# Moving the loads of V and of the weights from SyncE with casts on compute engines to casting DMAs issued by GpSimd

## The chip, the cores and the metric

One core of one Trainium2 chip. The metric is the device time of one execution in microseconds (us), the median over the executions of a run. Traces are of one profiled execution each. Seven of the fourteen traces (e3b, e4, e5, e6, e8, e9, e10) lack the records of 40 to 43 of the 1152 dense matmuls. Where a sum over all matmuls is quoted, it is of traces that have all 1152. Medians in the text are over all runs of a kernel; e2, e3 and e5 have one slow run of four, and for them the median of the fast three is given too.

## The reference

```python
q_d, k_d, v_d = (t.reshape(B, H, S // 4, 4, D).mean(axis=3) for t in (q, k, v))
out_up    = np.repeat(softmax_attention(q_d, k_d, v_d), 4, axis=2)     # pooled attention
mask      = np.abs(pos[:, None] - pos[None, :]) < 4
out_local = softmax(where(mask, scale * q @ k.T, -1e9)) @ v            # banded attention
x = (out_up + out_local).transpose(0, 2, 1, 3).reshape(B * S, H * D)   # 4608 x 512
h = x @ w_in                                                           # 512 x 2048
return (h - tanh(h)) @ w_out                                           # 2048 x 512
```

B = 8, H = 8, S = 576, D = 64. Inputs and output are float32; the kernel computes its matmuls in bf16. Heads are handled in pairs, 4 pairs to a batch, so 32 pairs: pairs 0 to 3 are batch 0, pairs 4 to 7 batch 1.

## The kernel before

The kernel records every piece of work as an operation (engine, estimated time, reads, writes, priority) and then lets its own scheduler place all of them, before the chip sees anything. So each engine's instruction order is fixed when the kernel is built. An operation with the keys it reads or writes is ordered after the ones that wrote them. `op("POOL", ...)` is GpSimd, `op("SP", ...)` is SyncE's queue, `op("DMA", ...)` stands for a transfer.

```python
def load(ns, fn, keys, cost, pri):
    op("SP", ns, fn, writes=list(keys) + ["queue", ("q", keys[0])], pri=pri)
    op("DMA", cost, None, reads=[("q", keys[0])], writes=keys, pri=pri)

def load_v(p):                     # V of a pair: two heads, 128 x 5 rows of 64 floats each
    ...
    for i in range(2):
        def issue(...):
            nc.sync.dma_start(out=t[:, i], in_=win(-4, 128, 5))       # t: fp32 staging tile
        load(1000, issue, [("vst", s, i)], T_V, -30)                  # a key for each head

def load_w(src, dst, name, f, stage, keys):                           # a 1 MB piece of weights
    ...                                                               # fp32 into borrowed space,
    load(600, issue, keys, T_W, -30)                                  # then four casts
    for c in range(4):
        P.choice([... for eng, ns, fn in CAST], reads=keys, writes=[(name, f, c)], ...)

def prep_v(p):                                                        # the cast of V
    P.choice([... tensor_copy(out=vw[w][:, 2 * jj:2 * jj + 2, :, 0:64], in_=vst[s]) ...],
             reads=[("vst", s, 0), ("vst", s, 1)], writes=[("vw", w, jj)], pri=10 * p - 12)

load_qk(0)
for p in range(NP):                # NP = 4 pairs of batch 0
    if p + 1 < NP:
        load_qk(p + 1)
    load_v(p)
...                                # then w_in; w_out between the loads of pairs 4 to 7
```

While PE (TensorE) would be idle before its first dense matmul, the emitter fills in matmuls on a constant tile ("filler"); these compute nothing.

The softmax here doesn't subtract the row's maximum and nothing guards it: scores larger than these inputs give would overflow.

## Time and profile before

| | before |
|---|---|
| median, 2 runs | 346.85 us (346.81 to 346.89) |
| profiled span (a further run, 345.75 us) | 343.9 us |
| first out-matmuls of pairs 0 / 2 | 17.55 / 24.61 us |
| first dense matmul | 30.45 us |
| first out-matmuls of pairs 4 to 7 | 46.8, 54.0, 61.4, 68.1 us |
| PE time without useful matmuls, to 50 us / to the end | 21.4 / 38.1 us |

"Out-matmuls" are those of attention probabilities with V (`ps_ox<-vw,E`); "dense" are the 1152 matmuls of 128x512 of the two weight layers. The last row is worked out from the trace: each matmul that isn't filler is counted at the time that its columns take (512 columns: 0.216 us, from runs of eight dense matmuls that take 1.73 us), and what is missing from the clock time is unused. Short matmuls take longer than their columns (the 320 out-matmuls take 63 ns each, 65 columns are 27 ns), so the absolute figures are too large.

From the page of the kernel before (busy us and share; busy tenths of 40 slices; the queue; instruction groups; an issue):

```profile
PE 322.8 (94%) x2502; PEld 162.9 (47%) x2502; DVE 225.0 (65%) x370; ACT 227.0 (66%) x368; POOL 155.1 (45%) x200
PE   4777999989999999989999799999999999999995
POOL 5644555646689625668976686783000000000000
q1 hardware_dynamic: 99278, 60.30, 68.0%
L351 POOL CAST vw<-vst 128x640 bf16<-128x640 f32 x32 | 26.2, 818 | 7.0 <-DMA vst<-in_v_dram 5.6
vst<-in_v_dram SPq DMA_DIRECT2D x62, 160.0 KB, 5.1
```

PE is nearly full from the fifth slice (34 us) to the end, so the time is PE's work plus what the first slices lose. V is cast 32 times on GpSimd for 0.82 us each; all data comes on one queue.

The timeline of PE before (start, length, what, and in brackets the idle time before it and what ended it):

```profile
17.55 0.33 PE L536 MATMUL ps_ox<-vw,E 128*128 128x65 bf16 x5
...
24.61 0.32 PE L536 MATMUL ps_ox<-vw,E 128*128 128x65 bf16 x5 [0.25 <-ACT vd L396]
...
30.45 2.75 PE L617 MATMUL ps_hy<-xT,w_in_sb 128*128 128x512 bf16 x12 [1.20 <-DVE xT L597]
```

V is there when PE wants it: none of these waits on it. Busy time by stretch in the crowded middle of the kernel (us PE, PEld, DVE, ACT, POOL, then granted clock, DMA share, GB/s):

```profile
100.00:220.00 120.00, 114.52 (x978) 57.92 (x977) 98.52 (x152) 98.35 (x150) 85.63 (x97) 1.00 1.01 223
```

GpSimd is busy 85.6 of 120 us, 71%.

### The profile page before, as it was taken

The numbers are of one execution on the slowest core, as the hardware profiler recorded it, in microseconds if no ns is written. First come the engines' busy times: TensorE is split into PE (matmuls) and PEld (weight loads), VectorE is DVE, ScalarE is ACT, GpSimd is POOL, SyncE is SP. The second block draws the span as 40 slices with busy tenths as digits, with TensorE's granted clock in tenths as the row PEclk, the third lists the DMA queues.
The fourth block names the chain that finished last, engine by engine and source line by source line (L and its number), as shares of the span: only waits on it lengthen the run. The fifth ranks groups of instructions, "written<-read, shape, count | busy, mean of one in ns | idle before, by whom it ended". The sixth has DMA issues, their size and how long they took to land.

```text
span 343.9 us, 6722 instructions
## 1 busy us (share of the span) xinstructions
PE 322.8 (94%) x2502; PEld 162.9 (47%) x2502; DVE 225.0 (65%) x370; ACT 227.0 (66%) x368; POOL 155.1 (45%) x200
## 2 busy tenths in 40 slices
PE   4777999989999999989999799999999999999995
PEld 2453555545565554434454344545444444444442
DVE  3787784579989878888887868876533433344300
ACT  2885996578878949878888687985443444344411
POOL 5644555646689625668976686783000000000000
PEclk9899999999999999999999999999999999999999
DMA  7999999985779884999999999834201000100021
GB/s 210 273 393 349 328 355 306 294 266 152 176 196 234 199 215 95 216 256 200 253 232 268 237 255 215 192 78 66 57 30 63 30 30 32 61 30 33 30 90 64
DMA packets 99310, 60.72 MB, mean 177 GB/s; under 512 B 77774, under 2 KB 82382, under 8 KB 99278
## 3 DMA queue, kind: packets, MB, share of 16 engines
q1 hardware_dynamic: 99278, 60.30, 68.0%
q8 instruction: 19, 0.31, 0.4%
q14 instruction: 13, 0.11, 0.1%
HBM read 42.46 MB, written 9.44 MB: 151 GB/s over the span
## 4 chain that ended last, share of the span: by engine, by line
PE 69%; DVE 8%; DMA 8%; issue 5%; POOL 4%; ACT 3%; SPq 2%; POOLq 0%; ACTq 0%; DVEq 0%
PE ps_hy L617 29%; PE ps_hy L644 29%; DMA qT<-qr 4%; PE ps_ts L476 2%; DVE ln L554 2%; PE ps_ox L536 2%; DMA vst<-in_v_dram 2%; DVE E L512 2%; PE ps_ts L441 2%; DMA qkn<-in_k_dram 2%; PE ps_ox L543 1%; SPq L291 1%; POOL half L457 1%; DMA lT<-ln 1%; PE ps_ox L389 1%
## 5 line engine op out<-in xcount | busy, mean ns | idle before, releaser
L617 PE MATMUL ps_hy<-xT,w_in_sb 128*128 128x512 bf16 x576 | 145.1, 379 | 1.2 <-DVE xT L597 1.2
L644 PE MATMUL ps_hy<-w_out_sb,gT 128*128 128x512 bf16 x576 | 142.6, 379 | 0.0
L628 DVE TENSOR_TENSOR gT<-ps_hy,u 128x512 bf16<-128x512 f32 x144 | 96.5, 686 | 65.8 <-ACT u L625 64.0
L625 ACT ACTIVATE u<-ps_hy 128x512 f32<-128x512 f32 x144 | 84.1, 601 | 67.8 <-PE ps_hy L617 67.3
L644 PEld LDWEIGHTS <-gT 128*128 128x128 bf16 x576 | 54.4, 98 | 63.3
L617 PEld LDWEIGHTS <-w_in_sb 128*128 128x128 bf16 x576 | 52.8, 98 | 59.8 <-issue 1.3
L457 POOL TENSOR_TENSOR half<-qk 128x576 f32<-128x576 bf16 x28 | 32.5, 1160 | 19.4 <-ACT qk L445 10.9
L432 ACT COPY qk<-qT 128x576 bf16<-128x576 bf16 x32 | 38.0, 1216 | 0.0
L509 ACT ACTIVATE E<-ps_ts 128x960 bf16<-128x960 f32 x32 | 30.9, 972 | 9.4 <-PE ps_ts L476 9.1
L554 DVE TENSOR_TENSOR ln<-ps_ox,r 128x896 bf16<-128x896 f32 x32 | 34.9, 1090 | 1.0
L416 POOL CAST qr<-qkn 128x576 bf16<-128x576 f32 x31 | 22.8, 735 | 24.7 <-PE ps_ts L441 11.1
L512 DVE TENSOR_TENSOR E<-E,mask 128x960 bf16<-128x960 bf16 x32 | 28.0, 879 | 8.2 <-ACT E L509 8.1
L655 ACT COPY y<-ps_hy 128x512 f32<-128x512 f32 x36 | 21.2, 589 | 17.9 <-PE ps_hy L644 17.6
L351 POOL CAST vw<-vst 128x640 bf16<-128x640 f32 x32 | 26.2, 818 | 7.0 <-DMA vst<-in_v_dram 5.6
L416 DVE CAST qr<-qkn 128x576 bf16<-128x576 f32 x32 | 23.7, 744 | 6.4 <-DMA qkn<-in_k_dram 3.9
L536 PE MATMUL ps_ox<-vw,E 128*128 128x65 bf16 x320 | 20.1, 194 | 3.3 <-DVE E L525 1.8
L462 POOL TENSOR_TENSOR qkd<-half 128x288 bf16<-128x288 f32 x30 | 21.4, 714 | 2.9 <-DVE r L552 1.7
L372 POOL TENSOR_TENSOR v<-v 72x512 f32<-72x512 f32 x16 | 20.9, 1309 | 1.2 <-DMA v<-in_v_dram 0.2
L536 PEld LDWEIGHTS <-E 128*128 128x128 bf16 x320 | 16.3, 98 | 10.8 <-DVE E L512 2.7
L445 ACT COPY qk<-ps_ts 128x1152 bf16<-128x1152 bf16 x16 | 18.0, 1126 | 3.9 <-PE ps_ts L441 3.9
L376 POOL TENSOR_TENSOR vp<-v 72x256 bf16<-72x256 f32 x16 | 11.7, 732 | 17.5 <-PE ps_ox L543 16.6
L476 PEld LDWEIGHTS <-qk 64*128 64x128 bf16 x320 | 10.2, 95 | 18.5 <-issue 16.9
(74 smaller groups left out, 260.2 us busy)
## 6 DMA issues: line engine op xcount, KB each, us to landing
vst<-in_v_dram SPq DMA_DIRECT2D x62, 160.0 KB, 5.1
qkn<-in_q_dram SPq DMA_DIRECT2D x32, 288.0 KB, 3.6
qkn<-in_k_dram SPq DMA_DIRECT2D x32, 288.0 KB, 4.5
out_dram<-y SPq DMA_DIRECT2D x36, 256.0 KB, 3.0
v<-in_v_dram SPq DMA_DIRECT2D x16, 288.0 KB
gT<-in_moe_w_in_dram SPq DMA_DIRECT2D x4, 1024.0 KB, 6.2
xT<-in_moe_w_out_dram SPq DMA_DIRECT2D x8, 256.0 KB, 6.4
gT<-in_moe_w_out_dram SPq DMA_DIRECT2D x2, 1024.0 KB, 8.1
```

The source lines that it names most:

```text
L351: P.choice([(eng, ns, lambda fn=fn: fn(out=vw[w][:, 2 * jj:2 * jj + 2, :, 0:64], in_=vst[s])) for eng, ns, fn in CAST_V[p >= NEARLY]], rea ...
L416: P.choice([(eng, ns, lambda dst=dst, srt=srt, fn=fn: fn(out=dst, in_=srt)) for eng, ns, fn in REORDER[p >= NEARLY][h]], reads=[("qkn", sn ...
L432: op("ACT", 600, lambda i=i: A.copy(out=full[:, i].rearrange("p (g a) -> p g a", a=A9), in_=qT[s].rearrange("p a (g i) -> p i g a", i=2)[: ...
L457: eng.tensor_tensor(out=half, in0=four[:, :, :, 0:2], in1=four[:, :, :, 2:4], op=ALU.add)
L509: op("ACT", 870, lambda: A.activation(out=e1, in_=ps[:, :, 0:480], func=AF.Exp, scale=SCALE), reads=ts, writes=[("E", s, 0)], pri=pri)
L512: op("DVE", 700, lambda: V.tensor_tensor(out=e1, in0=e1, in1=mask[:, 0:480].unsqueeze(1).to_broadcast([128, 2, 480]), op=ALU.mult), reads= ...
L536: T.matmul(po[:, hh, 65 * t:65 * t + 65], E[s][:, c:c + 128], vw[w][:, 2 * jj + hh, t, :], start=True, stop=True)
L554: op("DVE", 1010, lambda: V.tensor_tensor(out=ln[s].rearrange("p n (h d) -> p h n d", d=D), in0=blocks[:, :, :, 0:64], in1=r[s].unsqueeze( ...
L617: T.matmul(ps_hy[slot], w_in_sb[:, dc, fc * 128:(fc + 1) * 128], xT[dc][:, kb * 512:kb * 512 + 512], start=(dc == 0), stop=(dc == N_DC - 1))
L625: op("ACT", 490, lambda: A.activation(out=u[us], in_=ps_hy[slot], func=AF.Tanh), reads=[("hy", slot)], writes=[("u", us)], pri=-1)
L628: op("DVE", 620, lambda: V.tensor_tensor(out=gT[g][:, fc, :], in0=ps_hy[slot], in1=u[us], op=ALU.subtract), reads=[("hy", slot), ("u", us) ...
L644: T.matmul(ps_hy[slot], gT[g][:, fc, ts * 128:ts * 128 + 128], w_out_sb[:, fc, :], start=(fc == 0), stop=(fc == N_FF - 1))
```

## The change

The intent is to spare the casts of V and weights (26 us of GpSimd for V), the staging tiles, and half of the bytes that V and weights write, and to leave SyncE to q, k, transposes and stores. The Trainium skill (DMA: Bandwidth & Descriptors, SWDGE vs HWDGE vs iDMA) has a cast during a DMA as a feature of GpSimd-issued DMAs alone, so they all move to GpSimd's instruction order.

```diff
-    NQKN, NVST, NVW = 4, 5, 3
+    NQKN, NVW = 4, 4
-    vst = fixed("vst", [128, 2, NT, 64], FP32, NVST)
 ... load_v:
-                    nc.sync.dma_start(out=t[:, i], in_=win(-4, 128, 5))
+                    GP.dma_start(out=t, in_=win(-4, 128, 5))          # t: slice of bf16 vw
-            load(1000, issue, [("vst", s, i)], T_V, -30)
+            op("POOL", 1000, issue, writes=[("vw", w, jj), ("vq", p, i)], pri=10 * p - 40)
+            op("DMA", T_V, None, reads=[("vq", p, i)], writes=[("vw", w, jj)], pri=-30)
 ... load_w (w_out alike; the casts go):
+                GP.dma_start(out=dst[:, :, 512 * f:512 * f + 512],
+                             in_=src[:, 512 * f:512 * f + 512].rearrange(
+                                 "(c p) f -> p c f", p=128))
+        op("POOL", 1000, issue, reads=[("q", after)], writes=keys + [("wq", name, f)],
+           pri=W_PRI)
+        op("DMA", T_W, None, reads=[("wq", name, f)], writes=keys, pri=-30)
-    def prep_v(p): ...
 ... order of the loads:
+        load_w(moe_w_in, w_in_sb, "w_in", f, ("qkn", 3, 1))
 ...
+        if 0 <= nl[0] - NP - 1 < 4:
+            load_w(moe_w_out, w_out_sb, "w_out", nl[0] - NP - 1,
+                   ("qkn", (nl[0] - 1) % NQKN, 1))
```

Both heads of a pair now write the *same* key `("vw", w, jj)`, so to the scheduler the second head's load follows the landing of the first. And a weight may be issued as soon as a load of q and k has been *issued* (`("q", after)`).

More of the change, by code (lines that the diff above doesn't have):

```diff
@@ L296, in load_v @@
     def load_v(p):
-        b, j, s = p // NP, p % NP, p % NVST
-        t = vst[s]
+        b, j, w, jj = p // NP, p % NP, (p // 2) % NVW, p % 2
         for i in range(2):
@@ L302, in load_v @@
             base = v[b, h]
+            t = vw[w][:, 2 * jj + i, :, 0:64]
             def win(tok, n, nt, base=base):
@@ L306, in win, with issue @@
                                ap=[[D, n], [QW * D, nt], [1, D]])
-            def issue(h=h, i=i, win=win):
+            def issue(h=h, win=win, t=t):
                 if b == 0 and h == 0:
-                    nc.sync.dma_start(out=t[4:128, i, 0, :], in_=v[b, h, 0:124, :])
-                    nc.sync.dma_start(out=t[:, i, 1:5, :], in_=win(QW - 4, 128, 4))
+                    GP.dma_start(out=t[4:128, 0, :], in_=v[b, h, 0:124, :])
+                    GP.dma_start(out=t[:, 1:5, :], in_=win(QW - 4, 128, 4))
@@ L312, in issue @@
                 elif b == B - 1 and h == H - 1:
-                    nc.sync.dma_start(out=t[0:100, i, 4, :], in_=v[b, h, 476:576, :])
-                    nc.sync.dma_start(out=t[:, i, 0:4, :], in_=win(-4, 128, 4))
+                    GP.dma_start(out=t[0:100, 4, :], in_=v[b, h, 476:576, :])
+                    GP.dma_start(out=t[:, 0:4, :], in_=win(-4, 128, 4))
                 else:
-                    nc.sync.dma_start(out=t[:, i], in_=win(-4, 128, 5))
+                    GP.dma_start(out=t, in_=win(-4, 128, 5))
@@ L317, in load_v, with clear @@
             if (b, h) in ((0, 0), (B - 1, H - 1)):
-                def clear(h=h, i=i):
-                    part = t[0:32, i, 0, :] if h == 0 else t[96:128, i, 4, :]
+                def clear(h=h, t=t):
+                    part = t[0:32, 0, :] if h == 0 else t[96:128, 4, :]
                     V.memset(part, 0.0)
-                op("DVE", 100, clear, writes=[("vst", s, i)], pri=-99)
-            load(1000, issue, [("vst", s, i)], T_V, -30)
-    def load_w(src, dst, name, f, stage, keys):
+                op("DVE", 100, clear, writes=[("vw", w, jj)], pri=-99)
@@ L326, in issue, with load_w @@
+            op("POOL", 1000, issue, writes=[("vw", w, jj), ("vq", p, i)], pri=10 * p - 40)
+            op("DMA", T_V, None, reads=[("vq", p, i)], writes=[("vw", w, jj)], pri=-30)
+    def load_w(src, dst, name, f, after):
         def issue():
             if src is moe_w_in:
-                nc.sync.dma_start(out=stage.rearrange("p (c f) -> p c f", c=4),
-                                  in_=src[:, 512 * f:512 * f + 512].rearrange(
-                                      "(c p) f -> p c f", p=128))
-            else:
-                rows = src.rearrange("(f p) n -> p f n", p=128)
-                if isinstance(stage, list):
-                    for c in range(4):
-                        nc.sync.dma_start(out=stage[c], in_=rows[:, 4 * f + c, :])
-                else:
-                    nc.sync.dma_start(
-                        out=stage.rearrange("p (c f) -> p c f", c=4),
-                        in_=rows[:, 4 * f:4 * f + 4, :])
@@ L340, in load_w @@
-        load(600, issue, keys, T_W, -30)
-        for c in range(4):
-            part = stage[c] if isinstance(stage, list) else stage[:, 512 * c:512 * c + 512]
-            to = dst[:, c, 512 * f:512 * f + 512] if src is moe_w_in else dst[:, 4 * f + c, :]
-            P.choice([(eng, ns, lambda part=part, to=to, fn=fn: fn(out=to, in_=part))
-                      for eng, ns, fn in CAST], reads=keys, writes=[(name, f, c)],
-                     pri=W_PRI + f)
-    def prep_v(p):
-        s, w, jj = p % NVST, (p // 2) % NVW, p % 2
-        P.choice([(eng, ns, lambda fn=fn: fn(
-            out=vw[w][:, 2 * jj:2 * jj + 2, :, 0:64], in_=vst[s]))
-                  for eng, ns, fn in CAST_V[p >= NEARLY]],
-                 reads=[("vst", s, 0), ("vst", s, 1)],
-                 writes=[("vw", w, jj)], pri=10 * p - 12)
+                GP.dma_start(out=dst[:, :, 512 * f:512 * f + 512],
+                             in_=src[:, 512 * f:512 * f + 512].rearrange(
+                                 "(c p) f -> p c f", p=128))
+            else:
+                GP.dma_start(out=dst[:, 4 * f:4 * f + 4, :],
+                             in_=src.rearrange("(f p) n -> p f n", p=128)
+                             [:, 4 * f:4 * f + 4, :])
@@ L357, in load_v4 @@
+        keys = [(name, f, c) for c in range(4)]
+        op("POOL", 1000, issue, reads=[("q", after)], writes=keys + [("wq", name, f)],
+           pri=W_PRI)
+        op("DMA", T_W, None, reads=[("wq", name, f)], writes=keys, pri=-30)
     def load_v4(p):
@@ L683 @@
     M2_FIRST, T_DMA, X_DMA, NEW = 16, 16, 16, 16
-    ORDER = "p0p1p2p3"
     T_QK, T_V, T_W, W_PRI, NEARLY = 800, 1000, 2850, -3, NP
-    CAST = [("POOL", 700, GP.tensor_copy), ("ACT", 520, A.copy)]
-    CAST_V = [[("POOL", 720, GP.tensor_copy), ("ACT", 640, A.copy)],
-              [("POOL", 720, GP.tensor_copy)]]
     any3 = [("DVE", 600, V.tensor_copy), ("ACT", 650, A.copy),
@@ L724 @@
         load_v(p)
-    stages = []
-    for g in range(2):
-        t = gT[g].rearrange("p f c -> p (f c)").bitcast(FP32)
-        for e in range(2):
-            stages.append((t[:, 2048 * e:2048 * e + 2048],
-                           [("gT", g, 8 * e + c) for c in range(8)]))
-    for e in range(2):
-        stages.append(([xT[c][:, 2304 + 1024 * e:3328 + 1024 * e].bitcast(FP32)
-                        for c in range(4)],
-                       [("x", 4 + 2 * e, c) for c in range(4)]))
     for f in range(4):
-        load_w(moe_w_in, w_in_sb, "w_in", f, *stages[f])
-    queue = list(ORDER)
+        load_w(moe_w_in, w_in_sb, "w_in", f, ("qkn", 3, 1))
     nl = [NP]
     def load_next():
-        while queue and queue[0] != "p":
-            f = int(queue.pop(0))
-            load_w(moe_w_out, w_out_sb, "w_out", f, *stages[(4, 5, 2, 3)[f]])
-        if queue:
-            queue.pop(0)
         if nl[0] < NPAIR:
@@ L750, in load_next @@
             nl[0] += 1
-        if not queue or "p" not in queue:
-            while queue:
-                f = int(queue.pop(0))
-                load_w(moe_w_out, w_out_sb, "w_out", f, *stages[(4, 5, 2, 3)[f]])
-    for p in range(2):
-        prep_v(p)
+        if 0 <= nl[0] - NP - 1 < 4:
+            load_w(moe_w_out, w_out_sb, "w_out", nl[0] - NP - 1,
+                   ("qkn", (nl[0] - 1) % NQKN, 1))
     made = 0
@@ L770 @@
             pool_v(p // 2)
-        if p + 2 < NPAIR:
-            prep_v(p + 2)
         if p == 0:
```

## The prediction

> **What bounds it now.** TensorE. The matmul groups of the profile show 1152 128x512 dense matmuls; in the chain of waits a run of eight takes 1.73 us, so 0.216 us each and 249 us in all. The timeline has the first dense matmul at 30.45 us. Counting every matmul at its columns over the full clock, I find about 19 us of PE time not used before 30 us and only about 6 us from there to the end (near 70-80, 110-120, 150-160 and 190-200 us). The last 100 us are dense matmuls alone. So whatever the change frees on other engines can return some 6 us plus something of the start; what it delays at the start, or in the chains that feed PE between 40 and 235 us, is paid in full.
>
> **What it removes.** 32 V casts on GpSimd (26.2 us, 818 ns each), 24 weight casts (GpSimd 14 x about 0.63, ScalarE 10 x about 0.62: 15 us), the staging tiles. SyncE loses 76 DMA issues; in its queue one V issue takes about 0.58 us. Bytes read stay. None of the casts is near the end of the chain of waits; the V landing is 2% of it.
>
> **What it adds.** 66 V and 8 weight issues on GpSimd, in its instruction order. No trace here shows what one costs. The Trainium skill (DMA: Bandwidth & Descriptors, SWDGE vs HWDGE vs iDMA) says that such descriptors are computed in software on the GpSimd cores; a V load has 640 rows of 256 bytes. My estimate, a guess bounded by the hardware queue's 0.58 us, is 1 to 1.5 us of GpSimd each. Each pair of heads then trades 0.82 us of cast for 2 to 3 us of issue. From 100 to 220 us GpSimd is busy 72% of the time (busy time by stretch), 0.61 without V casts; at 7.5 us a pair, issues add 0.27 to 0.40. That is 88% to over 100%, on the engine that pools q and k (1.16 + 0.71 us) ahead of the scores. Each issue also waits until the casting DMA eight before it has landed, so early on weights hold up GpSimd's queue.
>
> **Start.** In the built order GpSimd issues the first V loads only after its constants (5.5 us), and the second head of pairs 0 and 1 comes after three 1 MB weight loads; that of pairs 2 and 3 after five. 2 KB packets take 85 ns, so 1 MB is 2.7 us on 16 engines; with q and k interleaved, V of pair 0 is whole at 22 to 25 us (before: cast by 14.5) and of pair 2 near 30. The built PE order has 38 filler matmuls in one stretch there. Dense work starts near 36 us instead of 30.45: +5.
>
> **Sum.** Start +5; middle +3 to +15 from GpSimd; gains from relieved ScalarE and from transposes no longer queued behind V: -2 to -4. Predicted 358 us, 8 in 10 between 348 and 378. Chances: faster 0.04, within 2% 0.28, slower 0.68.
>
> **Signs.** Right: first dense matmul at 34 to 38 us; long PE wait before the first out-matmuls (on V's landing); issue time of 1 us or more per casting DMA on GpSimd; PE waiting through scores on the q/k pooling adds between 100 and 235 us; dense-only tail near 100 us unchanged. Wrong: dense starts by 31 us; GpSimd issue near 0.3 us; PE unused after the start still 6 us.
>
> **What would make it wrong.** A cheap issue (then only the start costs, near 350); a dear one of 2 us or more (GpSimd-bound from 100 us, 375 and up); casting packets slower than 18 ns (256 B) or 85 ns (2 KB), delaying the start further; VectorE copies locking GpSimd out while it writes descriptors.

## The result and the profile after

| | before | after |
|---|---|---|
| median, 2 runs | 346.85 us | 365.61 us (365.04 to 366.18) |
| first out-matmuls of pairs 0 / 2 | 17.55 / 24.61 us | 30.94 / 41.15 us |
| first dense matmul | 30.45 us | 47.48 us |
| first out-matmuls of pairs 4 to 7 | 46.8 to 68.1 us | 66.3 to 82.9 us |
| PE time unused, to 50 us / to the end | 21.4 / 38.1 us | 35.9 / 57.3 us |

The ratio is 1.0557, 95% interval 1.0506 to 1.0608. Ratios here are the mean time of one kernel's fast runs over that of the other's in the same rounds, so not quite the ratio of the medians quoted. The spans differ by 363.1 - 343.9 = 19.2 us and so, as the useful matmuls are the same, does the unused PE time (57.3 - 38.1): 14.5 us of it arise before 50 us and 4.7 us later. Not all of this is idle time. The granted clock of TensorE was 0.74 from 30 to 40 us and 0.91 from 40 to 50 us, where before it was 1.00 in both. With PE busy 6.8 and 9.1 us of these stretches, an estimate from these figures is 0.26 x 6.8 + 0.09 x 9.1 = 2.6 us. Why the clock was lower there is not shown.

The same lines of the page, after:

```profile
PE 336.2 (93%) x2547; PEld 168.6 (46%) x2547; DVE 228.1 (63%) x374; ACT 220.2 (61%) x353; POOL 178.1 (49%) x224
PE   5895899999999999979898899999999999999995
POOL 8625685466679863689786896864000000000000
q1 hardware_dynamic: 52992, 41.43, 43.8%
q0 software_dynamic: 46224, 9.44, 30.8%
L315 POOL DMA_DIRECT2D vw<-in_v_dram x62 | 54.4, 881 | 20.0 <-PE ps_ox L520 7.8
vw<-in_v_dram POOLq DMA_DIRECT2D x62, 80.0 KB, 4.9
```

PE looks busier in the second and third slices than before; that is filler. One V issue holds GpSimd for 0.881 us (62 of them, 54.4 us), so GpSimd is now busier in all than with the casts (178.1 against 155.1 us). The Trainium skill (Perfetto Trace Analysis, DMA Instruction — SWDGE (GPSIMD)) says that such an instruction's end in the profile is the end of writing descriptors, not of the transfer. The trace agrees: the instruction is 0.881 us, the landing comes 4.9 us (median) after the issue. The queue of the casting DMAs carries V in packets of 128 bytes that took a median 32 ns (mean 33.5); before, V's packets of 256 bytes took a median 18 ns.

The timeline of GpSimd after, from its first DMA on:

```profile
5.46 0.71 POOL L309 DMA_DIRECT2D vw<-in_v_dram  x1
6.17 0.79 POOL L310 DMA_DIRECT2D vw<-in_v_dram  x1
6.93 2.58 POOL L315 DMA_DIRECT2D vw<-in_v_dram  x3
9.46 2.29 POOL L328 DMA_DIRECT2D w_in_sb<-in_moe_w_in_dram  x3
11.69 1.77 POOL L315 DMA_DIRECT2D vw<-in_v_dram  x2
14.49 0.76 POOL L328 DMA_DIRECT2D w_in_sb<-in_moe_w_in_dram  x1 [1.03 <-DMA vw<-in_v_dram]
16.93 0.74 POOL L332 DMA_DIRECT2D w_out_sb<-in_moe_w_out_dram  x1 [1.68 <-DMA vw<-in_v_dram]
20.53 0.84 POOL L315 DMA_DIRECT2D vw<-in_v_dram  x1 [2.86 <-DMA vw<-in_v_dram]
22.97 0.86 POOL L315 DMA_DIRECT2D vw<-in_v_dram  x1 [1.60 <-DMA w_in_sb<-in_moe_w_in_dram]
```

The first heads of pairs 0 to 3 go out, then three weights, then the second heads of pairs 0 and 1; those of pairs 2 and 3 come after five weights. The bracketed waits are a rule of this build: each casting DMA waits until the one eight before it has landed. The trace bears it out: none of the 66 issues with one eight places ahead starts less than 0.28 us after that landing. A casting DMA that is late to land therefore stops GpSimd, and everything behind it in GpSimd's order. Here the first three waits (1.03 to 2.86 us) are for first heads of V; the last (1.60 us) is the first behind a 1 MB weight, and more of that kind follow.

PE's timeline after, and the piece of the chain of waits (start, length, what) that ends where its second line begins:

```profile
18.03 8.38 PE L759 MATMUL ps_ox<-lT 128*128 128x512 bf16 x38
29.42 0.73 PE L373 MATMUL ps_ox<-vw,pick 128*128 128x256 bf16 x5 [3.01 <-DMA vw<-in_v_dram]
...
30.94 0.32 PE L520 MATMUL ps_ox<-vw,E 128*128 128x65 bf16 x5 [0.24 <-ACT vd L380]
...
47.48 1.47 PE L601 MATMUL ps_hy<-xT,w_in_sb 128*128 128x512 bf16 x6 [0.23 <-DVE xT L581]
```

```profile
12.52 16.85 DMA vw<-in_v_dram
```

38 filler matmuls and a wait of 3.01 us end with V: the second head of pair 1, issued at 12.52 us, lands 16.85 us later, behind three weights. In the middle:

```profile
100.00:220.00 120.00, 111.51 (x993) 56.84 (x991) 101.47 (x150) 93.97 (x147) 94.10 (x108) 1.00 1.11 199
```

GpSimd is busy 94.1 of 120 us (78%) and PE 3.0 us less than before.

### The profile page after: what moved, and what is told of

The parts are those of the page before. It is cut to its first block, busy times and chain, and to the rows that moved or that the text cites. A ratio compares the mean times of both kernels' runs of the same rounds, so it can differ in the third digit from the quotient of the medians.

```text
span 363.1 us, 6738 instructions
## 1 busy us (share of the span) xinstructions
PE 336.2 (93%) x2547; PEld 168.6 (46%) x2547; DVE 228.1 (63%) x374; ACT 220.2 (61%) x353; POOL 178.1 (49%) x224
## 4 chain that ended last, share of the span: by engine, by line
PE 66%; DVE 12%; DMA 9%; ACT 6%; POOL 3%; issue 3%; ACTq 0%; DVEq 0%; POOLq 0%
PE ps_hy L601 27%; PE ps_hy L628 27%; DMA vw<-in_v_dram 5%; DMA qT<-qr 3%; DVE ln L538 2%; ACT qk L416 2%; PE ps_ox L520 2%; PE ps_ts L460 2%; DVE gT L612 2%; DVE E L496 2%; PE ps_ts L425 2%; PE ps_ox L527 2%; DVE E L509 1%; PE ps_ox L373 1%; DVE xT L570 1%
## 5 line engine op out<-in xcount | busy, mean ns | idle before, releaser
L315 POOL DMA_DIRECT2D vw<-in_v_dram x62 | 54.4, 881 | 20.0 <-PE ps_ox L520 7.8
L400 POOL CAST qr<-qkn 128x576 bf16<-128x576 f32 x28 | 19.0, 682 | 12.8 <-PE ps_ts L425 9.3
L536 DVE RECIPROCAL r<-ps_ox 128x14 f32<-128x14 f32 x32 | 7.7, 241 | 22.6 <-PE ps_ox L527 21.8
L446 POOL TENSOR_TENSOR qkd<-half 128x288 bf16<-128x288 f32 x28 | 20.2, 722 | 0.9
```

What stands on the lines that cost most here:

```text
L315: GP.dma_start(out=t, in_=win(-4, 128, 5))
L400: P.choice([(eng, ns, lambda dst=dst, srt=srt, fn=fn: fn(out=dst, in_=srt)) for eng, ns, fn in REORDER[p >= NEARLY][h]], reads=[("qkn", sn ...
```

## The experiments

The first theory: the order of the loads at the start (V's second heads behind weights) costs most of the 19 us. Rivals: the work that the issues give to GpSimd in the middle; the slower packets; the weights' DMAs themselves.

### e7_order_alone: the kernel before, its loads in the order of after

```diff
+    for p in range(NP): load_qk(p)
+    for p in range(NP): load_v(p, (0,))            # first heads
+    w_in 0, 1, 2;  load_v(0, (1,)); load_v(1, (1,)); w_in 3, w_out 0; load_v(2, (1,)); load_v(3, (1,))
```

All by SyncE and cast as before. 

> The kernel before, nothing cast by DMA and all of it issued by SyncE, with the loads in the changed kernel's order: first heads, three weights, second heads of pairs 0 and 1, two weights, second heads of pairs 2 and 3. Theory: order alone costs. By packets of 85, 95 and 18 ns the last second head lands near 25 us instead of 17, so dense at 33 to 38 us, total 350 to 355 us; less than the changed kernel, since q and k of four more pairs and slower packets do not stand ahead of it here. Rival (order does not matter, the casting path does): within 1 us of before.

Measured: 354.31 us, ratio 1.0222 (1.0187 to 1.0257). Dense started at 43.69 us, the first outs at 28.1 us. The order alone gives 13 of the 17 us of late start, with no GpSimd DMA in the program, but only 8 of the 19 us of time. The time is in the range expected; the first dense matmul was to come at 33 to 38 us and came later.

### e1_v_first: a key for each head

```diff
-            op("POOL", 1000, issue, writes=[("vw", w, jj), ("vq", p, i)], pri=10 * p - 40)
+            op("POOL", 1000, issue, writes=[("vw", w, jj, i), ("vq", p, i)], pri=10 * p - 40)
```

(and the readers of `vw` read both keys). V of pairs 0 to 3 is then issued ahead of all eight weights. 

> The changed kernel with one key for each head of V, so that both heads of pairs 0 to 3 are issued ahead of all eight weight loads; every transfer still casts and is still issued by GpSimd. Theory (the start is lost because second heads of V stand behind weights in the same ring): out-matmuls of pair 0 start by 20 us instead of 30.9, the first dense matmul at 30 to 36 us instead of 47.5, total 347 to 354 us. Rival (the casting path itself is slow: V packets of 32 ns instead of 18, 0.88 us an issue): the first dense matmul stays after 41 us, total over 358 us.

Measured: 366.62 us, ratio 1.0596 (1.0559 to 1.0633): a miss. The first outs did come at 22.58 us instead of 30.94, yet dense started at 44.25. PE's and GpSimd's timelines of this run show why:

```profile
40.56 1.14 PE L425 MATMUL ps_ts<-ident,qr 128*128 128x128 bf16 x9 [7.39 <-POOL qr L400]
```

```profile
20.62 0.74 POOL L328 DMA_DIRECT2D w_in_sb<-in_moe_w_in_dram  x1 [2.48 <-DMA vw<-in_v_dram]
21.35 2.97 POOL L332 DMA_DIRECT2D w_out_sb<-in_moe_w_out_dram  x4
26.63 0.85 POOL L315 DMA_DIRECT2D vw<-in_v_dram  x1 [2.31 <-DMA w_in_sb<-in_moe_w_in_dram]
...
38.97 0.85 POOL L315 DMA_DIRECT2D vw<-in_v_dram  x1 [1.38 <-DMA w_out_sb<-in_moe_w_out_dram]
39.83 0.68 POOL L400 CAST qr<-qkn 128x576 bf16<-128x576 f32 x1
```

PE waits 7.39 us for a cast of q and k of pair 4 that takes 0.68 us. It stands in GpSimd's order behind V issues of batch 1, and each of those waits for one weight to land. All eight weights are still ahead of batch 1. So the theory was too narrow: it is not only which V is behind which weight, but what else is behind a blocked issue. Part of the loss may be the clock: PE was granted 0.54, 0.80 and 0.69 in the three stretches of 10 us from 20 to 50 us (before: 1.00 in each; e10 below: 0.57, 1.00 and 1.00). No run separates this from the waits.

### e2_w_only and e3_v_only: one half of the change each

e2: the kernel before with weights alone by casting DMAs (issued as early as in after). 

> The kernel before with its eight weight loads alone replaced by casting DMAs from GpSimd; V by SyncE with casts as before. Theory (order of V behind weights): V does not stand behind weights, so 343 to 351 us and dense from 29 to 34 us. Rival (casting weight loads take the DMA engines and hold GpSimd at the start): dense after 38 us, total over 355 us.

Measured: 357.84 us (fast runs 356.50), ratio 1.0302 (1.0230 to 1.0373), dense at 37.56 us: a miss. V still comes on SyncE's queue, and GpSimd's timeline shows it starved:

```profile
22.44 1.53 POOL L332 DMA_DIRECT2D w_out_sb<-in_moe_w_out_dram  x2
29.08 0.72 POOL L343 CAST vw<-vst 128x640 bf16<-128x640 f32 x1 [5.12 <-DMA vst<-in_v_dram]
```

The Trainium skill (DMA: Bandwidth & Descriptors, Queues, rings and completion order) says that each DMA engine goes round-robin between the queue rows it has work for, packet by packet. That would give weights on a second queue a share of the engines ahead of V already queued on the first, where on one queue V goes first. The trace agrees: from 14 to 24 us it has 1479 weight packets (1024 bytes written) on GpSimd's queue and 1460 V packets (256 bytes) on SyncE's, one for one. SyncE's queue moved 0.37 MB in these 10 us, against 3.41 MB before.

e3: the changed kernel with weights staged and cast as before, V alone by casting DMAs. 

> The changed kernel with the weights staged through SyncE and cast as before; V alone by casting DMA. Theory: no weights in V's ring, so the start is close to before (dense at 29 to 35 us), and what stays is the middle's loss of about 4 us: 348 to 355 us. Rival (V's casting DMAs are what costs the start): dense after 38 us, total over 357 us.

Measured: 390.27 us (fast runs 390.10), ratio 1.1227 (1.1148 to 1.1307), dense at 67.52 us, the first outs at 52.8: a miss, in the rival's range. The V issues of GpSimd stand between weight casts on the same engine, each waiting for its landing. It says little about V's casting as such, since it makes an order of its own.

### e3b_v_only_heads and e4_v_gp_plain

e3b is e3 with a key for each head. 

> e3 (V alone by casting DMA, weights staged by SyncE and cast) with one key for each head, so that second heads no longer stand behind casts of weights in GpSimd's order; that stand, not the DMA, is my reading of the 390 us of e3 (pool of pair 0 at 50.7 us). Theory: dense at 31 to 38 us, 348 to 357 us. Rival (V's casting DMA beside plain weights is slow): pool of pair 0 after 30 us, total over 365 us.

Measured: 370.91 us, ratio 1.0695 (1.0620 to 1.0770): the heads' keys give back 19 us, but outs of pair 2 come at 50.9 us, with the same mixture of weight casts and issues on GpSimd.

e4 is the kernel before with V issued by GpSimd *without* a cast and the casts kept; one look. 

> The kernel before with V issued by GpSimd but not cast: float32 into the staging tiles, casts kept. It measures two things: packets of V at 18 ns, as SyncE's, if the cast is what made them 32 ns (32 if GpSimd's queue is); and the issue time, 0.85 to 0.9 us again if the cast has no part in it (near 0.6 if it has). Total 350 to 365 us, since GpSimd now does both issue and cast.

Measured: 376.83 us, above the range expected (one run, so its state is unknown). One issue took 0.872 us (62), against 0.881 with the cast, so the cast has no visible part in the cost of an issue. Without a cast the records have V in merged packets (2048 of 4 KB at a mean 251 ns, the rest mostly of 2 KB) instead of 40,928 small ones, and the kernel is slower still; packet size alone doesn't order these runs.

### e5_spread: e1 with w_out, and V of batch 1, placed behind landings of w_in

```diff
+            after = ([] if p < NP else [("w_in", min(2 * (p - NP) + i, 3), 0)] if p < 2 * NP
+                     else [("vw", (p - 4) // 2 % NVW, jj, 1)])
 ...  w_out f only after w_in f has landed
```

> e1 (both heads of V of pairs 0 to 3 first) with each weight of w_out held in the order until one of w_in has landed, and V of pairs 4 to 7 placed behind, so that GpSimd's casts for pairs 4 and 5 no longer stand behind issues that wait for weights to land. e1 put the first out-matmuls at 22.6 us instead of 30.9 and then lost it: PE waited from 33 to 40.6 us for GpSimd's cast for pair 4, which stood behind six V issues. Theory (order: V behind weights, and GpSimd's compute behind issues that wait for the DMA eight before): first dense matmul at 31 to 37 us, total 348 to 355 us, of which 3 to 5 us over before from the middle. Rival (the casting path is inherently slow at the start): dense after 41 us, total over 359 us.

Measured: 364.32 us (fast runs 363.85), ratio 1.0500 (1.0424 to 1.0576): a miss that taught most. The start *was* mended: dense at 34.14 us, outs at 21.5. But V of batch 1 was now held behind w_in, and outs of pairs 4 to 7 came at 59.9 to 75.0 us (before: 46.8 to 68.1). An early first dense matmul is worth nothing if batch 1's attention, which must run between the dense blocks of batch 0, is late.

### e6_w_later: e2 with each weight held until V of a pair has landed

```diff
-        load_w(moe_w_in, w_in_sb, "w_in", f, ("qkn", 3, 1))          # after an issue
+        load_w(moe_w_in, w_in_sb, "w_in", f, [("vst", 2 + f // 2, f % 2)])   # after a landing
```

(w_out alike, behind V of pairs 4 to 7.) 

> e2 (weights alone by casting DMA) with each weight placed in GpSimd's order behind the landing of a pair's V, instead of all at 10 to 24 us. Theory (e2's loss is weights taking turns with q, k and V at the start): dense at 29 to 33 us, 343 to 349 us, the best of the casting versions. Rival (casting weights cost by themselves): 352 us or more, as e2.

Measured: 345.93 us, ratio 0.9991 (0.9930 to 1.0051), the same as before: as expected. The same eight casting DMAs cost 10 us in e2 (3.0% by the ratio) and nothing here. What differs is when they are issued, and with it the built order of every engine. "Held" here and below means held in the kernel's own scheduler.

### e8, e9 and e10: V by casting DMAs in part and in full, weights as in e6

All three have a key for each head. The theory by then was that V's casting DMAs cost in the first eight pairs only.

e8: V of pairs 8 to 31 by casting DMAs. 

> The kernel before with the weights cast by DMA at the times that cost nothing in the earlier run (345.9 us), and V of pairs 8 to 31 by casting DMAs of GpSimd, V of pairs 0 to 7 as before. Theory (what V's casting DMAs cost is paid while the first eight pairs are loaded and computed; later on the loads run ahead and GpSimd has room): 345 to 350 us, first dense matmul near 30 us, first out-matmuls of pairs 4 to 7 at 47 to 70 us as before. Rival (1.76 us of issues instead of 0.82 us of cast per pair on an engine busy 72% of the time, and packets of 32 instead of 18 ns, cost all through the middle): 352 to 360 us.

e9: V of pairs 0 to 7 by casting DMAs. 

> The mirror: V of pairs 0 to 7 by casting DMAs (each head by itself, ahead of the weights), V of the later pairs by SyncE and casts as before. Theory: 356 to 366 us, with out-matmuls of pairs 4 to 7 late (55 to 80 us instead of 47 to 68). Rival: 346 to 352 us.

e10: all V by casting DMAs. 

> The kernel after with V ahead of the weights and each weight behind the V of a pair: all V by casting DMAs. Theory: as the run with the first eight pairs alone, within 3 us, so 356 to 366 us; the three runs add up (this minus 345.9 is the sum of the other two minus 345.9) within 4 us. Rival that the order was the cause alone: 345 to 350 us. First dense matmul at 30 to 36 us under either.

| | median us | ratio (interval) | first outs | first dense | outs of pairs 4 to 7 |
|---|---|---|---|---|---|
| e8 | 353.04 | 1.0171 (1.0112 to 1.0229) | 17.5 | 30.91 | 45.6 to 63.8 |
| e9 | 345.90 | 0.9985 (0.9935 to 1.0035) | 22.3 | 37.08 | 36.2 to 59.5 |
| e10 | 348.19 | 1.0047 (1.0001 to 1.0094) | 22.1 | 37.53 | 36.8 to 58.7 |

The theory fell. e9 was to cost 10 us or more and costs nothing; e10 is within 1% of the kernel before, as its rival ("the order was the cause alone") had it. The three don't add up either: 2.3 us measured for e10 over 345.9, 7.1 + 0 from the others, outside the 4 us allowed. Only its first dense matmul was later than both expected (37.5 us, not 30 to 36).

e10 differs from e1 in one working respect: when a weight may be issued (it also keeps staging tiles that nothing uses). GpSimd's timeline in e10:

```profile
6.95 6.82 POOL L344 DMA_DIRECT2D vw<-in_v_dram  x8
14.33 0.85 POOL L344 DMA_DIRECT2D vw<-in_v_dram  x1 [0.56 <-DMA vw<-in_v_dram]
16.44 0.85 POOL L344 DMA_DIRECT2D vw<-in_v_dram  x1 [1.25 <-DMA vw<-in_v_dram]
20.17 2.54 POOL L344 DMA_DIRECT2D vw<-in_v_dram  x3 [2.88 <-DMA vw<-in_v_dram]
22.71 0.68 POOL L445 CAST qr<-qkn 128x576 bf16<-128x576 f32 x1
23.31 1.52 POOL L363 DMA_DIRECT2D w_in_sb<-in_moe_w_in_dram  x2
```

V of batch 0 and of most of batch 1 goes out before the first weight, and the cast of q and k for pair 4, which in e1 came at 39.83 us, runs at 22.71. PE in e10:

```profile
20.02 1.23 PE L418 MATMUL ps_ox<-vw,pick 128*128 128x256 bf16 x5 [3.23 <-DMA vw<-in_v_dram]
...
36.83 0.47 PE L565 MATMUL ps_ox<-vw,E 128*128 128x65 bf16 x5
...
37.53 1.03 PE L646 MATMUL ps_hy<-xT,w_in_sb 128*128 128x512 bf16 x3
```

Dense work starts 7 us later than before, but pair 4's out-matmuls come 10 us *earlier* (36.83 against 46.84): PE spends the time on attention that it would otherwise do later. A late first dense matmul is a loss only if PE has nothing else. And the chain of waits and the busy time by stretch of e10:

```profile
8.63 11.25 DMA vw<-in_v_dram
```

```profile
100.00:220.00 120.00, 114.91 (x919) 57.01 (x934) 97.66 (x149) 96.43 (x151) 93.47 (x108) 1.00 0.99 195
```

GpSimd does the same work as in after (62 V issues of 0.880 us, 93.5 us busy in this stretch against 94.1), V's packets are as slow (median and mean 32 ns), and PE is at least as busy as before the change (114.9 against 114.5, though records are missing). So in e10 GpSimd's work and the slow packets together cost 1.5 us by the medians, and 3.3 us (0.94%) at the upper end of the interval. That is a net figure: what the spared casts and the new order give back is in it.

e8's 353 us lies in the range of the rival that it was to refute. Its gap to e9 is 2.3 us at the first of the 36 output copies (at 81 us), 4.4 us at the 9th (at 156 us), 8.0 us at the 17th (at 227 us) and 7.1 us at the last, so most of it arises in the middle, where e10 does the same V loads with little loss. What in e8's built order does that was not found; it stays open.

### e11_after_w_later: the changed kernel, its weights alone moved

```diff
-        op("POOL", 1000, issue, reads=[("q", after)], ...
-        load_w(moe_w_in, w_in_sb, "w_in", f, ("qkn", 3, 1))
-                   ("qkn", (nl[0] - 1) % NQKN, 1))
+        op("POOL", 1000, issue, reads=[after], ...
+        load_w(moe_w_in, w_in_sb, "w_in", f, ("vw", 1, f // 2))
+                   ("vw", (nl[0] - 1) // 2 % NVW, (nl[0] - 1) % 2))
```

> The kernel after with one thing changed: each weight's issue is held, in the kernel's scheduler, until the V of a pair has landed (both heads of a pair still share a key). Theory (the moment at which the eight weights enter GpSimd's order, ahead of V, is the whole loss, and the work of GpSimd and slower packets none of it): 346 to 353 us, out-matmuls of pairs 4 to 7 before 65 us. Rival (the second heads, which still wait for the first heads, cost a part of it too): 355 to 364 us.

Measured: 353.11 us, ratio 1.0193 (1.0122 to 1.0265). That is 0.1 us above the theory's range, and below the rival's; outs of pairs 4 to 7 came at 39.5 to 58.8 us, as the theory had said. PE time unused: 27.2 us to 50 us, 46.3 us to the end, from a complete trace. GpSimd's timeline has the first weight behind 16 issues of V, with no wait listed:

```profile
23.05 1.74 POOL L315 DMA_DIRECT2D vw<-in_v_dram  x2
24.77 2.99 POOL L328 DMA_DIRECT2D w_in_sb<-in_moe_w_in_dram  x4
```

With e1, after and e10 it makes a square of two causes (ratios to the kernel before):

| | weights issued early | weights held behind V's landing |
|---|---|---|
| one key for both heads | after: 1.0557 | e11: 1.0193 |
| a key for each head | e1: 1.0596 | e10: 1.0047 |

Moving the weights is worth 12.5 us by itself (365.6 to 353.1), and 18.4 us where the heads have their own keys (366.6 to 348.2); these are medians of different rounds. The keys are worth nothing by themselves and 5 us once the weights are moved. No version beats both kernels: the best, e9 and e6, equal the kernel before within their intervals.

## Why the prediction was right or wrong

The direction, the range (348 to 378) and the cause of the late first outs (V's second heads behind three and five weights) were right. Two terms of the sum were mis-sized: the start was much too small, and the middle was put on the wrong mechanism.

- **"Start +5".** The first dense matmul came at 47.48 us, not near 36: +17.0; in unused PE time, 14.5 us to 50 us. V of pair 0 was to be whole at 22 to 25 us; its second head landed at 28.8, and that of pair 1, which PE waited for, at 29.4. I had taken packets at their speed before, though I named slower ones as a risk (V: 32 ns median for 128 bytes against 18 for 256); and I had followed V's landing but not what stands *behind* blocked issues: the second heads of pairs 2 and 3, issued at 20.5 and 23.0 us, and casts of q and k. e7 shows that the order alone makes 13 of the 17 us.
- **"Middle +3 to +15 from GpSimd".** This is the step that failed. I put GpSimd at 88% to over 100% from 100 to 220 us; it was 78% (94.1 of 120), as an issue took 0.88 us and not 1 to 1.5. PE's unused time after 50 us rose by 4.7 us, which is inside +3 to +15, but none of it is listed as the wait on pooled q and k that I had given as the reason. e10, with GpSimd just as busy (93.5 of 120) and the same 62 issues, is 17 us faster than after. The load on GpSimd was not the cause of the loss; the built order was. What makes the 4.7 us of the middle was not shown.
- **"Gains -2 to -4".** No run shows them by themselves. e6 takes the weights' casts away and gains nothing (0.9991), so at least the relief of ScalarE and GpSimd from those casts shows no net gain. It fits the waits of PE before, of which only 0.3 us from 50 to 235 us are on ScalarE.
- **Signs.** Right: the wait before the first outs ended by V's landing (38 filler matmuls and 3.01 us), and a tail of dense work alone unchanged (from the last other matmul to the end 105.1 us after, 104.1 before). Wrong: dense at 34 to 38 us, issues of 1 us or more, and PE waiting for pooled q and k in the middle: in 50 to 235 us after, no such wait is listed. Of the risks, "casting packets slower" came true but was nearly free in e10; V issues took 845 to 939 ns through the whole kernel, while VectorE worked 63% of the time, so no slowing of the issues beside VectorE's work was seen.

The sum came within 8 us of the result because a start that was too small stood beside a middle that was too large (+9 in its centre, 4.7 measured); that closeness is luck. What is settled: of the 19 us, moving the weights behind V alone gives back 12.5 us, and a key for each head as well gives back 17.4 us (365.6 to 348.2). Since every engine's order is rebuilt when a key changes, these runs compare whole built orders; how much of the gain is fewer blocked GpSimd instructions, how much is PE's new order (pairs 4 and 5 ahead of dense) and how much a higher clock is not separated.

## What to carry to other kernels

When DMAs move to a compute engine, the instruction order of that engine becomes the order of the loads, and every wait of a DMA issue stops the compute behind it. Cost such a change by walking the built order of that engine (what is issued before what, and what stands behind a blocked issue) before adding up busy time. Put big loads behind the small ones that the next stages need, by a dependence on their landing rather than on an issue; and judge a start by the useful work PE finds, not by when one kind of matmul begins.

## What the Trainium skill lacked or had wrong

- DMA: Bandwidth & Descriptors, SWDGE vs HWDGE vs iDMA, says that software writes the descriptors but not for how long an issue holds GpSimd; elsewhere the page calls generating them "small, variable" and gives about 1 us to the first byte. Here it was 0.88 us for 640 rows, 0.75 to 0.79 us for a 1 MB weight of 512 rows and 0.71 us for 124 rows, so mostly fixed; with and without a cast alike (0.881 and 0.872 us).
- The same page gives no time for casting packets. Here 128 bytes written from 256 read took a median 32 ns (18 ns for 256 bytes without a cast), and 1024 from 2048 a median 98 ns (85 ns for 2048 bytes without a cast, over all packets of that size).
- The same page, Issuing engines are not separate DMA queues, says that issuing on several engines saves only the issue time. It does not say what a second queue can cost: the same weights' DMAs from GpSimd cost 10 us or nothing (ratios 1.0302 in e2, 0.9991 in e6), by when they entered it.
- No page that I found has the wait for the casting DMA eight before, which in this build stopped GpSimd eight times in the first 50 us after the change: three times behind V (1.0 to 2.9 us) and five times behind weights (1.3 to 2.0 us).
